# Attention and MoE on one core: the clip of the weight words on one engine, a second product buffer, and a new written-out order

## The chip, the cores and the metric

One core of one Trainium2 chip runs the whole program in one launch. The metric is device time in microseconds of one execution; the kernel before has a median of 686.51 us over 3 runs (685.51 to 687.27).

## The reference, cut to what matters

Rotary attention on 4 batches x 8 heads x 576 tokens x 64 dimensions, and then a two-layer MoE-like block on all 2304 tokens, with a sigmoid gate:

```python
q_rot, k_rot = rotate(q), rotate(k)                     # halves rotated by cos/sin of position
scores = scale * q_rot @ k_rot^T                        # (4, 8, 576, 576)
attn = exp(scores - max); attn /= sum + 1e-9
x = (attn @ v).transpose(0, 2, 1, 3).reshape(2304, 512)
h = x @ w_in                                            # (2304, 2048)
g = h / (1 + exp(-1.702 * h))
out = g @ w_out                                         # (2304, 512)
```

w_in and w_out are float64 in DRAM. The kernel reads them as pairs of 32-bit words and builds float32 values from them on the chip.

## The kernel before, in words

**Work.** The 32 heads are taken as 16 pairs (two heads of 64 dimensions fill the 128 partitions). For each pair, `scores` (L650) makes five steps of score products on TensorE (PE); `softened` takes each 128x576 row block through a scaling with row minimum on VectorE (L681, engine DVE), an exp on ScalarE (L684, ACT) and, from pair 4 on, a transpose on DVE (L689); `weighted` (L756) multiplies with v in two parts of 144 small matmuls each. Pairs 0 to 3 use other forms (`weighted_whole`: transposes L795 on PE, products L820 to L833). Results go to DRAM (`x_dram`), split into a high and a low float32r part.

**Weights.** `weight` (from L864) runs 32 times, 16 column blocks of w_in and 16 row blocks of w_out. Each run is a chain on one [128, 2, 512] buffer CW: L894 and L896 on ACT (low word to integer, absolute value of the high word), the clip L898 (a `tensor_scalar` with max and min), L900 and L903 on DVE (shift, sign), L906 on GpSimd (engine POOL; adds the low bits), then a rounding copy (L908) and a subtraction (L909).

**MoE.** Tokens go in 9 chunks of 256. For chunks 0 to 4 `moe` does, for each of 16 column blocks f: 12 matmuls "M" (L939) into one PSUM buffer h of the pool PT, tanh on ACT (L945), (t+1)h on DVE (L947), the high part g on ACT or POOL (L949), the low part on DVE or POOL (L951), and 2 x 3 matmuls "O" (L956) with w_out that accumulate in SPS buffer 2. Chunks 5 to 8 go in two calls of `two_chunks` (L1087, L1128), which shares products between two chunks. In the kernel before h always takes PT buffer 1 of two, and t and g have one buffer each (T=1, G=1 in SLOTS).

**Order.** Every step is an `Op` of a `Plan` of 3050 steps. Nothing is scheduled at run time: `PLACES` gives each step's place in one stream, `ENGINES` the engine of each step that may run on more than one (A, V, G for ACT, DVE, POOL), and `Plan.order` sorts by place and hands out buffers in that order. Each engine runs its part of the stream strictly in order, and SyncE (SP) issues nearly all DMAs in order too. `COST` holds prices in ns that went into such an order and do nothing at run time: a POOL step with one 128x512 source stands there at 121 + 0.97 x 512 = 618. One more wait is added by hand at the end of the loop: each POOL step that uses the port shared with DVE waits for the DVE step with the port mark that precedes it in the stream (`holder`).

Of the kernel before, what the change touches and what calls it, by code (L numbers as in the profile page):

```python
# [38 lines left out]
PLACES = [18, 0, 55, 26, 17, 23, 22, 12, 34, 1, 14, 52, 37, 28, 36, 35, 13, 24, 25, 30, 9, 6, 44, 10, 11, 45, 27, 57,  # L39
# [287 lines left out]
def attention_moe(ctx: ExitStack, tc: tile.TileContext, q, k, v, w_in, w_out, cos_sin, out):  # L327
# [589 lines left out]
    def moe(c, fs, t0, step):  # L917
# [9 lines left out]
        last = [None, None]  # L927
        for f_i in fs:
            pr = t0 + (f_i - fs[0]) * step
            h, t, g = plan.buf("PT", (1,)), buf("T"), buf("G")  # L930
            terms = [[(kk, 0, 0) for kk in range(KD)], [(kk, 1, 0) for kk in range(KD)],
                     [(kk, 0, 1) for kk in range(KD)]]
            if f_i == fs[-1]:
# [315 lines left out]
```

## Time and profile before

| what | us |
|---|---|
| median of 3 runs | 686.51 |
| the profiled execution, its own time | 684.21 |
| its span from the first to the last instruction | 682.5 |
| PE busy | 642.7 (94%) |
| DVE busy | 501.2 (73%) |
| ACT busy | 344.6 (50%) |
| POOL busy | 306.2 (45%) |

The stretches of the span are: warm-up matmuls (0 to 12), pairs 0 to 4 without MoE work (12 to 118), pairs 4 to 9 beside the MoE products of the first chunks and the last weights (118 to 300), pairs 9 to 15 beside the rest of chunks 2 to 4 (300 to 507), and the two shared calls (507 to the end). Busy time of PE is time in which some matmul was in flight, so a PE that is busy all the time may still run below its rate; the number of matmuls in a stretch tells how much work was in it. A wait is listed as "who <- for whom".

### The profile page before, as it was taken

What the parts mean: (1) busy time and instruction counts of PE and PEld (TensorE: products, weight loads), DVE (VectorE), ACT (ScalarE), POOL (GpSimd) and SP (SyncE); (2) the same over time, 40 slices, a digit from 0 to 9 for tenths busy, and PEclk for the clock granted to TensorE, in tenths of its full rate; (3) what the DMA queues carried; (4) which work ended last, traced back from release to release, by engine and by line L of the source; (5) the groups of instructions that cost most, each with busy time, mean ns of one, the idle gap of its engine ahead of it and who ended that gap; (6) DMA issues with size and microseconds to landing.
All of it is one profiled execution on the core that took longest, in us unless ns stands there. A gap on an engine that the chain in (4) does not pass through costs nothing.

```text
span 682.5 us, 18292 instructions
## 1 busy us (share of the span) xinstructions
PE 642.7 (94%) x7258; PEld 529.5 (78%) x7258; DVE 501.2 (73%) x1104; ACT 344.6 (50%) x839; POOL 306.2 (45%) x329
## 2 busy tenths in 40 slices
PE   8999887889889899989999999999999999999997
PEld 7655555767667687778878888888799899889886
DVE  4998779778799998877878988688375466544442
ACT  3987678265767655534354546446234323332232
POOL 3454547263566648654555557443012243133242
PEclk9999769889999999999999999999999999999999
DMA  7638464775688857666556747555446442343301
GB/s 194 151 81 202 122 189 142 207 143 182 170 225 230 225 136 218 194 181 168 175 147 178 192 138 214 137 137 153 139 163 202 148 149 89 124 130 118 124 0 63
DMA packets 82994, 107.16 MB, mean 157 GB/s; under 512 B 41254, under 2 KB 60892, under 8 KB 79708
## 3 DMA queue, kind: packets, MB, share of 16 engines
q1 hardware_dynamic: 81852, 105.73, 54.2%
q8 instruction: 57, 0.93, 0.6%
q10 hardware_dynamic: 1056, 0.26, 0.2%
q14 instruction: 29, 0.24, 0.1%
HBM read 71.68 MB, written 23.91 MB: 140 GB/s over the span
## 4 chain that ended last, share of the span: by engine, by line
PE 63%; DVE 17%; ACT 6%; issue 5%; POOL 3%; DMA 3%; SPq 1%; DVEq 0%; POOLq 0%; ACTq 0%
PE SPS L1128 13%; PE PT L939 12%; PE SPS L956 11%; PE SPS L650 7%; PE PT L1087 6%; PE SPS L1087 6%; PE SPS L756 5%; DVE TP L681 3%; DVE TP L689 2%; ACT TP L684 2%; POOL CW L898 2%; DVE CW L903 1%; PE SPS L443 1%; PE PT L795 1%; DMA XS<-r_dram 1%
## 5 line engine op out<-in xcount | busy, mean ns | idle before, releaser
L939 PE MATMUL PT<-XC,win 128*128 128x256 f32 x960 | 137.0, 289 | 5.9 <-DVE T L947 4.9
L939 PEld LDWEIGHTS PT<-XC,win 128*128 128x128 f32 x960 | 123.9, 190 | 21.9 <-DVE T L947 11.7
L956 PE MATMUL SPS<-wout,G 128*128 128x512 f32 x480 | 134.5, 407 | 4.0 <-DVE G L396 2.0
L684 ACT ACTIVATE TP<-TP,ST 128x576 f32<-128x576 f32 x144 | 111.0, 772 | 35.6 <-DVE TP L681 35.4
L681 DVE TENSOR_SCALAR_CACHE_REDUCE TP<-SPS 128x576 f32<-128x576 f32 x144 | 103.6, 747 | 19.5 <-PE SPS L650 19.0
L956 PEld LDWEIGHTS SPS<-wout,G 128*128 128x128 f32 x480 | 83.1, 190 | 26.1 <-DVE G L396 4.9
L1128 PE MATMUL SPS<-wout,G 128*128 128x512 f32 x384 | 97.0, 394 | 0.0
L689 DVE STREAM_TRANSPOSE TP<-TP 128x576 f32<-128x576 f32 x108 | 79.5, 760 | 2.2 <-ACT TP L684 2.1
L387 POOL TENSOR_SCALAR G<-T 128x256 fp32r<-128x256 f32 x64 | 28.5, 446 | 116.1 <-PE SPS L956 40.4
L1128 PEld LDWEIGHTS SPS<-wout,G 128*128 128x128 f32 x384 | 69.0, 188 | 13.0 <-ACT O L391 0.4
L396 POOL TENSOR_TENSOR G<-T,G 128x256 fp32r<-128x256 f32 x75 | 56.2, 753 | 50.2 <-DVE T L1119 13.8
L756 PE MATMUL SPS<-TP,VR 32*64 32x144 f32 x3456 | 62.9, 290 | 7.8 <-issue 6.4
L945 ACT ACTIVATE T<-PT 128x256 f32<-128x256 f32 x80 | 30.5, 381 | 78.6 <-PE PT L939 54.6
L906 POOL TENSOR_TENSOR CW<-CW 128x512 int32<-128x512 int32 x32 | 41.1, 1285 | 61.9 <-DVE CW L903 22.4
L756 PEld LDWEIGHTS SPS<-TP,VR 32*64 32x64 f32 x3456 | 55.9, 133 | 15.0 <-issue 9.2
L384 ACT CAST G<-T 128x256 fp32r<-128x256 f32 x80 | 32.2, 405 | 42.5 <-DVE T L947 14.0
L650 PE MATMUL SPS<-KH 64*128 64x288 f32 (+1 forms) x216 | 47.2, 345 | 5.4 <-DVE TP L681 5.0
L947 DVE SCALAR_TENSOR_TENSOR T<-T,PT 128x256 f32<-128x256 f32 x80 | 32.6, 407 | 22.9 <-ACT T L945 22.8
L1119 DVE SCALAR_TENSOR_TENSOR T<-T,U 128x256 f32<-128x256 f32 x64 | 28.3, 452 | 28.3 <-ACT T L1117 27.9
L650 PEld LDWEIGHTS SPS<-KH 64*128 64x128 f32 (+1 forms) x216 | 27.3, 189 | 20.5 <-DVE TP L681 10.1
L1117 ACT ACTIVATE T<-U 128x256 f32<-128x256 f32 x64 | 25.8, 417 | 34.2 <-DVE U L396 17.5
L898 POOL TENSOR_SCALAR CW<-CW 128x512 f32<-128x512 f32 x17 | 32.6, 1917 | 19.8 <-DVE RQ L396 4.6
(132 smaller groups left out, 1153.9 us busy)
## 6 DMA issues: line engine op xcount, KB each, us to landing
TR<-t_dram SPq DMA_DIRECT2D x16, 1024.0 KB
VR<-VR SPq DMA_DIRECT2D x36, 288.0 KB
x_dram<-XS SPq DMA_DIRECT2D x16, 576.0 KB
XC<-x_dram SPq DMA_DIRECT2D x18, 512.0 KB
OW<-in_moe_w_in_dram SPq DMA_DIRECT2D x16, 512.0 KB
OW<-in_moe_w_out_dram SPq DMA_DIRECT2D x16, 512.0 KB
RQ<-in_k_dram SPq DMA_DIRECT2D x40, 142.0 KB
RQ<-in_q_dram SPq DMA_DIRECT2D x40, 142.0 KB
```

The lines of the kernel that those rows point to most:

```text
L396: return engine[e].tensor_tensor(to, a, b, op=how)
L650: nc.tensor.matmul(ss[h].t[:, c, 0:HALF], of[x][rows, S + t * 128:S + t * 128 + 128], of[y][rows, c * HALF:c * HALF + HALF], start=(m == 0 ...
L681: o = vec("DVE", "psum", S, lambda e: nc.vector.tensor_scalar(tile_to(), src(), by, LARGEST, op0=ALU.mult, op1=ALU.min, accum_out=st.t[:, ...
L684: o = vec("ACT", "sbuf", S, lambda e: nc.scalar.activation(to(), to(), AF.Exp, bias=st.t[:, 0, t:t + 1], scale=-1.0, accum_out=st.t[:, 1, ...
L689: return o, vec("DVE", "psum", S, lambda e: nc.vector.transpose(to(), to()), o, bufs=[tp], prio=prio + at["exp"] + at["across"])
L756: nc.tensor.matmul(bank[64 * h:64 * h + 64, 0:144], vr.t[rows, h, a], of()[rows, a, 144 * h:144 * h + 144], start=(a == 0), stop=(a == n_k ...
L898: o = vec("DVE POOL", "sbuf", DM, lambda e, a=a: engine[e].tensor_scalar(a(), a(), clip[0], clip[1], op0=ALU.max, op1=ALU.min), o, bufs=[c ...
L906: o = vec("POOL", "two", DM, lambda e, a=a, r=r: nc.gpsimd.tensor_tensor(a().bitcast(I32), a().bitcast(I32), r(), op=ALU.add), o, low, buf ...
L939: nc.tensor.matmul(h.t[:, 0:CT], win[f_i // KH][:, wl, kk, f_i % KH * 128:(f_i % KH + 1) * 128], xc[xl].t[:, kk, :], start=(i == m == 0), ...
L956: nc.tensor.matmul(acc.t[:, m, :], g.t[:, a, m * 128:(m + 1) * 128], wout[f_i // KH][:, b, f_i % KH, :], start=(f_i == fs[0] and i == 0), ...
L1087: nc.tensor.matmul(h(to), w(a)[:, k], x(b)[:, k], start=(begin and n == 0), stop=(n == 5), skip_group_check=True)
L1128: nc.tensor.matmul(acc[j].t[:, m, :], g.t[:, x, m * 128:(m + 1) * 128], wout[f_i // KH][:, y, f_i % KH, :], start=(begin and n == 0), stop ...
```

## The change

Four edits. The clip L898 is issued on DVE in all 32 runs of `weight` (17 of them were on POOL). The MoE product h may take either of the two PT buffers instead of buffer 1 alone. The pool T gets two buffers instead of one. PLACES and ENGINES are replaced as a whole. No step is added or removed, and the line numbers stay.

```diff
-PLACES = [18, 0, 55, 26, 17, 23, 22, 12, 34, 1, 14, 52, 37, 28, 36, 35, 13, 24, 25, 30, 9, 6, 44, 10, 11, 45, 27, 57,
...
+PLACES = [10, 0, 38, 8, 4, 17, 7, 52, 20, 28, 55, 1, 41, 36, 29, 22, 15, 16, 14, 6, 23, 30, 9, 18, 5, 19, 43, 37, 44,
...
-SLOTS = dict(SPS=3, PT=2, RAW=2, RAW1=1, BT=1, KP=0, KH=1, KL=1, ST=2, CS=1, XS=1, XC=4, T=1, G=1, O=2, OW=2, CW=2, TP=1, VR=1)
+SLOTS = dict(SPS=3, PT=2, RAW=2, RAW1=1, BT=1, KP=0, KH=1, KL=1, ST=2, CS=1, XS=1, XC=4, T=2, G=1, O=2, OW=2, CW=2, TP=1, VR=1)
...
-        o = vec("DVE POOL", "sbuf", DM, lambda e, a=a: engine[e].tensor_scalar(
+        o = vec("DVE", "sbuf", DM, lambda e, a=a: nc.vector.tensor_scalar(
             a(), a(), clip[0], clip[1], op0=ALU.max, op1=ALU.min), o, bufs=[cv], prio=prio)
...
-            h, t, g = plan.buf("PT", (1,)), buf("T"), buf("G")
+            h, t, g = plan.buf("PT"), buf("T"), buf("G")
```

What the two pairs of lists say, counted step by step (sorting the steps by PLACES gives each engine's order, the letters of ENGINES its steps):

| steps | before | after |
|---|---|---|
| clip L898 on DVE / POOL | 15 / 17 | 32 / 0 |
| wide rope multiplication L516 on DVE / POOL | 14 / 2 | 9 / 7 |
| flat rope, L570 to L574, on DVE / POOL | 38 / 22 | 32 / 28 |
| high part of g, L949, on ACT / POOL | 48 / 32 | 56 / 24 |
| low part of g, L951, on DVE / POOL | 36 / 44 | 45 / 35 |
| weight differences L991 on DVE / POOL | 19 / 13 | 12 / 20 |
| copies out of PSUM in `two_chunks` L1095 on ACT / DVE | 46 / 18 | 33 / 31 |
| products M that follow the product before them with no other PE step between (of 79) | 0 | 37 |
| pairs O that start with three products M issued ahead of them (of 80; otherwise one or two) | 0 | 26 |
| PE steps between the two parts of `weighted` for pair 8 | M1.12, a transpose, half an O | half an O |

A stretch of PE's order around pair 8 (S: score step, M f.a to c: thirds of a product, O f.x and y: halves, V: a part of `weighted`, I: the transpose of the sums):

```
before: S8.4 M1.10c O1.9y O1.9x M1.11a M1.11b M1.11c O1.10x O1.10y V8.0 M1.12a M1.12b M1.12c I8 O1.11y V8.1 O1.11x S9.0
after:  S8.4 O1.9x M1.11c M1.12a M1.12b M1.12c O1.10x O1.10y V8.0 O1.11y V8.1 I8 O1.11x S9.0
```

Of the DVE steps that stand ahead of S9.0 in the stream, the after list has 17 more at L898 and 5 fewer at L516, and at the other lines between 2 fewer and 2 more each.

## Rows read from the trace of the kernel before

**Rows 1.** The page: busy shares, then PE's granted clock in 40 slices.

```profile
PE 642.7 (94%) x7258; PEld 529.5 (78%) x7258; DVE 501.2 (73%) x1104; ACT 344.6 (50%) x839; POOL 306.2 (45%) x329
...
PEclk9999769889999999999999999999999999999999
```

**Rows 2.** Windows: length, busy PE, PEld, DVE, ACT, POOL (instructions), clock, DMA.

```profile
12.00:118.00 106.00, 93.35 (x631) 58.88 (x629) 91.01 (x213) 85.97 (x202) 57.34 (x45) 0.92 0.56 149
118.00:300.00 182.00, 163.78 (x2448) 132.93 (x2449) 160.76 (x334) 105.10 (x247) 104.20 (x87) 0.97 0.72 197
300.00:507.00 207.00, 203.34 (x3051) 173.85 (x3051) 155.56 (x344) 93.35 (x235) 91.69 (x106) 1.00 0.58 163
...
160.00:200.00 40.00, 34.65 (x384) 27.25 (x387) 33.81 (x72) 26.08 (x61) 24.43 (x17) 1.00 0.72 206
200.00:250.00 50.00, 45.46 (x782) 36.13 (x766) 47.79 (x94) 32.95 (x77) 25.87 (x19) 1.00 0.72 201
...
650.00:675.00 25.00, 25.00 (x138) 21.60 (x137) 10.50 (x26) 7.32 (x20) 11.19 (x19) 1.00 0.03 11
```

**Rows 3.** Weight loads in 160 to 200, by line: L939, L956, L650, L756.

```profile
160.00:200.00 40.00, 12.22 (x99) 1.00 0.72 206
...
160.00:200.00 40.00, 8.01 (x48) 1.00 0.72 206
...
160.00:200.00 40.00, 4.67 (x54) 1.00 0.72 206
...
160.00:200.00 40.00, 2.81 (x185) 1.00 0.72 206
```

**Rows 4.** Chain of waits where PE is dense: start, us, what.

```profile
305.67 2.44 PE SPS L756 x144
...
492.24 1.39 PE SPS L956 x6
493.62 1.43 PE PT L939 x12
```

**Rows 5.** DVE's waits, first from 118 to 300, then whole: us, times, longest.

```profile
DVE CW L900 <- POOL CW L898: 9.2, 8, 1.8
...
DVE CW L900 <- POOL CW L898: 12.8, 10, 2.1
```

**Rows 6.** Timeline of DVE, then POOL: start, us, engine, line [idle before <- releaser].

```profile
160.41 1.40 DVE L900 TENSOR_SCALAR CW<-CW 128x512 int32<-128x512 int32 x1
...
169.70 0.43 DVE L900 TENSOR_SCALAR CW<-CW 128x512 int32<-128x512 int32 x1 [1.78 <-POOL CW L898]
...
160.09 1.44 POOL L906 TENSOR_TENSOR CW<-CW 128x512 int32<-128x512 int32 x1 [3.86 <-DVE G L396]
...
167.74 1.92 POOL L898 TENSOR_SCALAR CW<-CW 128x512 f32<-128x512 f32 x1 [2.31 <-DVE win L396]
```

**Rows 7.** The clip and rope by line and form: count, ns min/median/max; then groups, mean.

```profile
L898 POOL TENSOR_SCALAR CW<-CW x17: 1915/1917/1924, 20.5 to 232.9; 128x512 f32<-128x512 f32 x17
L898 DVE TENSOR_SCALAR CW<-CW x15: 414/426/1233, 24.1 to 245.3; 128x512 f32<-128x512 f32 x15
...
L898 DVE TENSOR_SCALAR CW<-CW 128x512 f32<-128x512 f32 x15 | 8.9, 596 | 1.3 <-ACT CW L896 1.3
...
L396 DVE TENSOR_TENSOR BT<-RAW,CS 128x512 f32<-128x512 f32 (+1 forms) x16 | 8.5, 534 | 5.0 <-DMA CS<-in_cos_sin_dram 5.0
```

**Rows 8.** Waits of PE's weight loads, whole span.

```profile
PEld PT L939 <- DVE T L947: 11.7, 18, 1.9
```

**Rows 9.** Timeline of PE: `weighted` for pair 4; a score step and its follower.

```profile
118.68 6.30 PE L756 MATMUL SPS<-TP,VR 32*64 32x144 f32 x278 [0.35 <-DVE TP L689]
128.22 0.48 PE L756 MATMUL SPS<-TP,VR 32*64 32x144 f32 x10 [3.24 <-issue]
...
313.98 0.40 PE L650 MATMUL SPS<-KH 64*128 64x288 f32 x2
...
314.98 1.66 PE L956 MATMUL SPS<-wout,G 128*128 128x512 f32 x6
```

More of the change, by code (lines that the diff above doesn't have):

```diff
@@ L38 @@
 MORE_TIMES = ['T_AT']
-PLACES = [18, 0, 55, 26, 17, 23, 22, 12, 34, 1, 14, 52, 37, 28, 36, 35, 13, 24, 25, 30, 9, 6, 44, 10, 11, 45, 27, 57,
[160 rows of a table removed]
-ENGINES = (".......................................VVV.A.VVV.VVV.VVV.A.........................A.A.A.A.A.A.A.A.A"
-           ".AA.AA..AA..A..VAV..GGG.V.VVG.AAA.VVG.A.........................V.A.A.A.A.A.A.A.A.AA.AA..AA..A..VVG."
-           ".VGV.A.VVG.AVA.GVV.A.........................V.A.A.V.A.A.A.V.A.AV.AV..VA..A..GVG..VVG.A.VGV.VAV.VVV."
-           "V.........................A.A.A.A.A.V.A.A.A.AA.AA..AA..A..GAG..VVG.A..VGG.V.V.V..VVV.A.............."
-           ".......................VVAV..A..VAV..VGV.A..VVV.V.A.V..VVV.A.....................................AAA"
-           "V..V..GAG..VGV.VV.VVV.AVAVAV....................................AVAV..A..GAG..GGG.AV.VVV.AVAVAV....."
-           "...............................AAVA..V..GAG..GVV.AV.VVV.AVAGAV....................................AA"
-           "AA..A..GVG..VGG.AG.GVV.VVVVVG....................................AAAV..A..GAV..GGG.AV.VGV.VVAGAV...."
-           "................................AAAA..A..VAV..VVG.AG.VVV.AVVVVG....................................V"
-           "AAA..V..GAG..GGG.VV.VVV.AVAGAV....................................AVAA..A..GAG..GVV.AG.VVV.VVVGVV..."
-           ".................................AAAA..V..GAG..GVG.AV.VVV.AVVVAV...................................."
-           "AAAA..V..GAG..VGG.AG.VGV.VVVVVV....................................AVVV..A..VAV....V...AV...V...AV.."
-           ".V...AG...V...AG...G...VG...G...AV...V...AV...V...AV...G...AV...V...VV...G...VV...G...AG...V...AG..."
-           "V...AG...G...AV...G...VV...V...AV...G...AV...G...AV...G...AG...V...AV...G...AV...G...AV...G...AV...V"
-           "...AV...G...AV...V...AV...G...AV...G...AG...G...AG...V...AV...V...AV.......GG.......GG.......AG....."
-           "..GG.......AG.......AV.......AV.......AV.............AV.......AV.......AV.......AV.......AG.......AV"
-           ".......AV.......AV.............AG.......AG.......AG.......AV.......AV.......AV.......AV.......AV...."
-           "...........AG.......GG.......GG.......AV.......AG.......AG.......AG.......AG...............AG......."
-           "GG.......GV.......AG.......GG.......AV.......GG.......GG.......GG.......GV.......AV.......AG.......A"
-           "G.......GV.......GG.......AG.............AG.......AV.......AV.......GG.......GG.......GG.......AG..."
-           "....GV.......GG.......AG.......GG.......GG.......GV.......AG.......GG.......GG.............GG......."
-           "GG.......AV.......GG.......AV.......GG.......GG.......AV.......AV.......AV.......GV.......GV.......G"
-           "V.......AV.......AV.......AV......GVVVGGAG.AV.VGGGGGAG.AV.GGVVVVVG.AG.GVVVVVVG.AG.GGGVVVAV.AV.VGVGVG"
-           "AG.AG.GGGGGGAV.AG.VVVVVVAG.AG.......VVVAVVVVAGVVAVVVVV..A.A.A..V..V......GV....AG....GV....GG....A.A"
-           ".A..G..A......AV....AV....GV....AG....A.A.A..V..A......GV....GG....AV....AV....V.A.A..G..A......AG.."
-           "..AG....AV....AG....V.V.A..G..V......AV....GV....GV....AG....A.A.A..V..A......GV....AG....GV....GV.."
-           "..V.A.A..G..A......AV....AV....GG....AV....A.A.A..G..V......GV....AG....AV....AV..A.A.V.V.......GVGV"
-           "VVVVAVGVAVGVAV..A.V.A..G..A......GV....GG....AV....AG....V.A.A..V..A......GG....GG....AG....GG....A."
-           "A.A..G..V......GV....GG....GV....AG....V.A.A..G..A......GV....AG....GG....GV....A.V.V..G..V......AG."
-           "...AV....GV....AV....V.A.A..V..V......AG....AV....GG....GG....V.A.A..G..A......AG....AG....GG....AG."
-           "...V.A.A..G..A......GV....GG....GV....GG..V.A.A.A.")
@@ L231 @@
-SLOTS = dict(SPS=3, PT=2, RAW=2, RAW1=1, BT=1, KP=0, KH=1, KL=1, ST=2, CS=1, XS=1, XC=4, T=1, G=1, O=2, OW=2, CW=2, TP=1, VR=1)
+PLACES = [10, 0, 38, 8, 4, 17, 7, 52, 20, 28, 55, 1, 41, 36, 29, 22, 15, 16, 14, 6, 23, 30, 9, 18, 5, 19, 43, 37, 44,
[160 rows of a table added]
+ENGINES = (".......................................VVV.A.VVV.VVV.VVV.A.........................A.V.A.A.A.A.A.A.V"
+           ".VA.AA..AA..V..VVV..VVG.A.VGG.AVA.VGG.V.........................A.V.A.A.A.A.A.A.A.AA.AA..AV..A..VAG."
+           ".GGV.A.GGG.VAV.GGV.A.........................A.A.A.V.A.V.A.A.A.VA.AV..AA..A..GAG..VVV.A.VVV.AAA.GVV."
+           "V.........................A.A.A.A.A.A.A.A.A.AA.AA..AA..A..GAG..GGG.A..VVV.V.V.V..VVV.A.............."
+           ".......................VVAA..V..VAV..GVV.V..VVG.A.V.V..GVV.V.....................................AVV"
+           "A..V..GAG..GGV.AV.VVV.AVVGAV....................................AAAV..V..GAG..GGG.AV.VVV.AVAVAG....."
+           "...............................AAAV..A..GAG..VGV.AV.VVV.AVVVAV....................................AV"
+           "AV..A..GAG..GGG.AV.VVV.AVAVAV....................................AAAV..V..GAG..GGG.AG.GVV.AVAVAV...."
+           "................................AAAA..A..GAV..VGG.AG.GGG.AVVVVV....................................A"
+           "AVA..A..GAG..VGG.AV.VVV.VVAGAV....................................AAVA..A..GVG..VVV.AG.VVV.AVVVAV..."
+           ".................................AVAA..V..GAG..GGG.AG.GVV.VGVVAG...................................."
+           "VVAV..A..GAG..VGG.AV.VGG.AGVGVG....................................VVAA..A..VVV........VG.......VV.."
+           ".....AV.......AG.......AG.......AV.......AV.......AV.......VV.......AV.......AV.......AV.......AV..."
+           "....AV.......AG.......VV.......AV.......AV.......AV.......AG.......AV.......AV.......AV.......AV...."
+           "...AV.......AV.......AG.......AV.......AG.......AG.......AV.......AV.......AG.......GV.......AG....."
+           "..GG.......AV.......AV.......AV.......AV.............AV.......GV.......AG.......AG.......AG.......AV"
+           ".......AV.......AV.............AG.......AG.......GG.......AV.......AV.......AV.......AV.......AV...."
+           "...........AG.......AG.......GG.......AV.......AG.......GV.......AV.......AG...............AV......."
+           "AV.......AG.......AV.......AV.......AG.......GG.......AG.......GV.......AV.......AV.......GG.......A"
+           "V.......AG.......AG.......GV.............GV.......AV.......AV.......AV.......AG.......GG.......AV..."
+           "....AG.......AG.......AG.......GG.......AV.......AV.......AG.......AV.......GG.............GG......."
+           "GG.......GV.......GG.......AG.......GG.......GV.......AV.......AG.......GV.......GV.......GV.......G"
+           "V.......AV.......AV.......AV......GGGGGGAG.AV.GGGGGGVG.AG.VGGVGVAV.VV.GVVVVGVV.AG.VGGGVVAV.AV.VGVVGG"
+           "AG.AG.GGGGGVAV.AV.VVGVVGAG.VV.......VVVAVVVVVVVVAVVVAV..A.A.A..G..A......AV....AV....GV....AG....A.V"
+           ".A..V..A......GV....AV....AG....GG....V.V.A..V..A......GG....GV....GG....GG....V.A.A..G..V......AG.."
+           "..AG....AG....GV....A.V.V..G..V......GG....GV....AV....AV....A.V.A..V..A......AV....AG....GV....AV.."
+           "..V.V.A..G..A......AV....AG....AV....GV....A.V.A..V..A......AG....GV....AV....GG..V.V.A.A.......GGVV"
+           "GGGVAVVVAGVGAV..V.V.V..V..A......AV....GG....AG....AV....V.V.V..V..V......GG....AG....AG....AV....V."
+           "V.A..V..A......GG....AG....GV....AG....A.V.V..V..V......GG....AG....GG....GV....A.A.A..V..A......GV."
+           "...GG....GV....GG....V.A.V..G..A......GV....AG....AV....AG....A.V.A..V..V......AG....GG....AV....AV."
+           "...V.V.A..V..V......GG....GV....GG....GV..V.A.A.A.")
```

320 rows, old and new, of the table PLACES are left out of this document.

## The prediction, on record before the changed kernel ran

> **What bounds the kernel now.** I read the page's busy shares first [rows 1]: PE is busy 94% of a span of 682.5 us, and the clock line shows nine full slices in ten; of the five slices from 68 to 154 us four are below 9 tenths. A busy PE need not be at its rate, so the windows come next, stretch by stretch [rows 2], and then the work in a stretch against its length. From 650 to 675 PE is busy 25.00 of 25 us, and in the dense middle a product M of 12 matmuls takes 1.43 us, an O-half pair of 6 takes 1.39, 144 small ones of `weighted` 2.44 [rows 4], and 12 score matmuls stand from 313.98 to 314.98, 1.0 us [rows 9]. With these prices the counts of 160 to 200 [rows 3] are 99 x 0.119 + 48 x 0.232 + 54 x 0.083 + 185 x 0.0169 = 11.8 + 11.1 + 4.5 + 3.1 = 30.5 us of work in 40 us. So there PE loses 9.5 us, though its busy row says only 5.35 is idle. In 118 to 300 DVE is busy 160.8 of 182 us (88.3%), in 200 to 250 47.8 of 50 (95.6%); PE is idle 18.2 us there, but 3.7 from 300 to 507, where DVE is at 75% [rows 2]. I conclude: before 300 us the in-order DVE sets the pace and PE waits for what it makes; after 300 PE itself is the bound.
>
> The waits of DVE say what keeps it from being full. In 118 to 300 it stands idle 21.2 us (182 - 160.8), and 9.2 of them, 8 times, are one wait: the shift L900 for the clip L898 on POOL; 12.8 over the whole span [rows 5]. The timeline shows how one comes about [rows 6]: POOL begins a clip at 167.74, after having idled 2.31 us for a DVE step, takes 1.92, and DVE stands 1.78 before L900 at 169.70.
>
> **The change, part by part.**
>
> Clip on DVE. Seventeen clips of 1917 ns leave POOL (32.6 us of POOL time) and cost DVE 426 ns each, 7.2 us in all [rows 7]. What is late next behind a clip is DVE itself, with no hand-over: L900 follows in its own queue. So the wait for POOL goes: 9.2 us in the stretch that DVE bounds. A clip on DVE can now wait for ACT's absolute value (L896), with everything behind it in DVE's queue; the trace has 1.3 us of that for 15 clips [rows 7], so 1.3 x 17 / 15 = 1.5 for all; it stays inside the bounds below.
>
> Port. The mean of DVE's clips is 596 ns against a median of 426, with one of 1233 [rows 7]; L900 once took 1.40 us, beside a POOL step that ran from 160.09 for 1.44 [rows 6], against 0.43 elsewhere. By the mean the 17 clips cost 10.1 us instead of 7.2. The other bound: POOL loses 17 of its longest steps, and whatever DVE time they stretched comes back; a like 2.9 us. I take zero between them.
> The Trainium skill, "SBUF — State Buffer", section "SBUF: two separate sides", says that VectorE and GpSimd share one pair of ports as an exclusive lock: the one that starts first keeps it for its whole instruction, and a VectorE instruction in a two-port mode or with two SBUF inputs is then fully blocked. The stretched L900 agrees. The rule speaks against the clip on DVE, since it makes 17 more instructions that can be blocked, and by it alone the dearer 10.1 us would stand.
>
> Other engine letters. Ahead of S9.0, the first score step of pair 9, DVE gets 17 clips more (7.2), 5 rope multiplications L516 fewer (5 x 0.534 = 2.7, [rows 7]), and the rest of the lines nearly cancel; I put them at +0.8, with two either way. DVE's work there is 5.3 us more. The later letters (L951 on DVE 9 times more, L991 7 times fewer, L1095 13 more) fall in stretches in which DVE has 25% and more to spare [rows 2]: nothing, unless PE's density breaks there.
>
> Second product buffer and T=2. With one buffer each, M(f+1) waits until L947 has read h of f. That is 11.7 us in 18 waits of PE's weight loads [rows 8]. In the new order 37 of 79 products follow the one before directly, and 26 times three are issued ahead. With g still in one buffer, an O pair can't come sooner; the freedom is that PE has a product to do while DVE is late. It can't make a DVE-bound stretch shorter than DVE's work, so I don't add it to the sum; it is why I trust PE to follow DVE's gain. Bounds: 0 and -11.7.
>
> Order. SP's queue and the early stretch are newly ordered. In 12 to 118 DVE is busy 91.0 and ACT 86.0 of 106 us, and PE at a mean clock of 0.92 [rows 2]. Clip waits of 12.8 - 9.2 = 3.6 us lie outside 118 to 300 [rows 5], and half of the new DVE clips would be 3.6 us of work: no change, bounds -4 and +4. After 300: bounds -3.7 (all idle gone) and +3.5 (a stall more like the 3.24 us of rows 9). The last 176 us: no change.
>
> Sum. If DVE runs 118 to 300 at the share that 200 to 250 shows, its 160.8 + 5.3 us take 166.1 / 0.956 = 173.7 us, 8.3 less than 182. The bounds are work against waits alone, 5.3 - 9.2 = -3.9, and, with half of PE's 11.7 on top of the 8.3, -14. I take -8.3, since the 95.6% row still has POOL clips in it [rows 7]. 684.21 - 8.3 = 675.9 for an execution like the profiled one (span 674.2). That one lies 2.3 us under the median of the runs, so 678.2 in the median.
>
> **The rivals.**
>
> *More comes along.* The new lists also win in the stretches that I hold still: 4 us before 118, 3.7 after 300: 8.3 + 7.7 = 16, or 670.5. For it: PE has 12.7 us idle in 12 to 118 besides its low clock. Against: DVE and ACT are both above 80% there, and their work is the same.
>
> *Code stalls eat it.* In pair 4, where both parts of `weighted` stand back to back, PE stood 3.24 us at "issue" after 278 of 288 matmuls [rows 9], waiting for nothing that the profile shows. The new order leaves only half an O between the parts of pair 8. Two such stalls at 3.24 are 6.5; the gain falls to 1.8 us, 684.7: the same. Against: pair 4 stands nearly so in both lists, and other parts are spaced. The Trainium skill, "Runtime: NRT & Kernel Launch", section "Instruction fetch mechanics", has the sequencer refill its code block by block in the background, mostly hidden; by that this rival has no price, but the 3.24 us are there.
>
> *DVE inherits the wait (slower).* Its queue is in order, so with 17 clips more it may only stand elsewhere: before L896, before the stretched POOL additions L906, before exps. Its share then stays at 88.3%, and 166.1 us of work take 188.1: 6.1 longer than now, 692.6. It decides where DVE's share of 118 to 300 stays below 166.1 / 182 = 91.3%. Against: in 200 to 250, where POOL still ran clips up to 232.9 us [rows 7], it reached 95.6%.
>
> *The clip was slack.* Transfers, not DVE, time the stretch to 300, and the gain turns into another wait: 686.5. For it: DVE's share looks full only where several chains meet; against: 9.2 of 21.2 idle us have one cause.
>
> **How the numbers follow.** The forecast 0.50 (its own range 674 to 683), more 0.18, code stalls 0.10, slack 0.08, DVE inherits 0.14. The range 668 to 690 takes in the first four and the milder half of the slower case; below it lies 0.08, above it 0.09. About 0.3%, 2.1 us, is what a measurement can tell: faster means under 684.4, same up to 688.6. Faster: 0.47 + 0.18 + 0.05 + 0.02 = 0.72. Slower: 0.11 + 0.03 = 0.14. Same: the rest, 0.14.
>
> **What would show it.** Right: no wait of L900 for L898; POOL busy near 280; DVE above 93% from the start of M0.0 to about S10; M's wait for L947 well below 11.7; the dense tail starts some 8 us before 507. Wrong: DVE's share unchanged with new waits before L898 or L906 (it inherits), more "issue" before L756 (code), or the same gap between the first M and the tail with DMA at its end (slack). If the gain lies before 118 us, the sum is right by luck.

## The result, and the profile after

The changed kernel takes 661.39 us in the median of 4 runs (658.38 to 663.25), against 686.01 (685.07 to 687.27) for the kernel before on the same chip: a ratio of 0.9636 [0.9596, 0.9676]. The forecast was 678.2 with a range from 668 to 690, so the sign was right and the time lies below the range. The profiled execution took 663.25 against 684.21 before, 21.0 us less.

The page of the changed kernel, first the busy shares, then the granted clock [rows 1]:

```profile
PE 628.3 (95%) x7258; PEld 523.9 (79%) x7258; DVE 501.8 (76%) x1133; ACT 341.5 (52%) x830; POOL 277.4 (42%) x309
...
PEclk9999998999999999999999999999999999999999
```

POOL is at 277.4, near the 280 forecast, and DVE at 501.8 does no more than the 501.2 of before, although it runs 17 clips more. Windows of the changed kernel, in the stretches and columns of [rows 2]:

```profile
12.00:118.00 106.00, 92.47 (x811) 59.77 (x811) 101.45 (x233) 87.61 (x203) 51.98 (x50) 0.97 0.60 165
118.00:300.00 182.00, 169.40 (x2533) 143.30 (x2514) 160.09 (x352) 108.37 (x256) 84.09 (x78) 0.99 0.76 204
300.00:507.00 207.00, 206.06 (x2953) 177.61 (x2952) 157.76 (x351) 97.57 (x250) 93.01 (x103) 1.00 0.56 160
160.00:200.00 40.00, 38.02 (x515) 31.07 (x513) 39.21 (x88) 28.35 (x68) 21.46 (x20) 1.00 0.80 211
200.00:250.00 50.00, 47.13 (x575) 39.54 (x573) 47.65 (x104) 34.79 (x81) 29.22 (x28) 1.00 0.79 208
```

In 160 to 200 DVE went from 33.81 to 39.21 of 40 us. In 12 to 118, held still in the forecast, it went from 91.01 to 101.45 of 106.

These windows lie at fixed times, while the work moves to earlier ones. So I also take the time at which PE begins the same product in each trace (matmuls counted along PE's written order) and cut the span there: the first MoE product M0.0, the first score step of pair 9 (S9.0), and the first product of the shared calls (the tail).

| us, in the profiled execution | M0.0 starts | S9.0 starts | tail starts | span |
|---|---|---|---|---|
| before | 129.0 | 278.5 | 507.6 | 682.5 |
| after | 121.2 | 259.0 | 486.7 | 661.5 |
| after, second chip (changed_again) | 121.4 | 258.1 | 483.8 | 658.6 |

By stretch, from before to after: start -7.8, M0.0 to S9.0 -11.7, S9.0 to the tail -1.4, tail -0.1; on the second chip -7.6, -12.8, -3.4 and -0.1. The forecast had 0, -8.3, 0 and 0. Windows cut at these marks, before:

```profile
0.00:129.00 129.00, 111.27 (x987) 75.83 (x988) 106.15 (x238) 91.03 (x210) 64.08 (x62) 0.92 0.58 156
129.00:278.50 149.50, 136.45 (x1892) 109.72 (x1890) 132.08 (x277) 90.17 (x211) 82.52 (x68) 0.98 0.73 196
278.50:507.60 229.10, 223.86 (x3320) 190.78 (x3321) 174.93 (x385) 106.26 (x267) 109.08 (x121) 1.00 0.59 166
```

And after:

```profile
0.00:121.20 121.20, 104.33 (x988) 70.62 (x988) 108.08 (x245) 90.86 (x207) 54.48 (x58) 0.97 0.61 166
121.20:259.00 137.80, 129.44 (x1898) 108.39 (x1891) 129.68 (x284) 89.84 (x210) 63.98 (x60) 1.00 0.81 212
259.00:486.70 227.70, 223.49 (x3319) 191.79 (x3320) 173.78 (x386) 106.33 (x272) 109.41 (x115) 0.99 0.59 168
```

Up to S9.0 DVE is busy 106.15 + 132.08 = 238.2 us before and 108.08 + 129.68 = 237.8 after. It is idle for 40.3 us before (278.5 - 238.2) and 21.2 after. So nearly all of the 19.5 us gained by then is idle time of DVE that is gone (19.1). Its waits from 118 to 300 in the changed kernel, the answer to [rows 5]:

```profile
DVE TP L681 <- PE SPS L650: 7.8, 7, 4.8
DVE CW L898 <- ACT CW L896: 2.9, 3, 1.7
DVE win L396 <- ACT win L384: 1.8, 1, 1.8
```

The wait of L900 for the clip is no longer there. What is late next, ACT's absolute value, costs 2.9 us. Two lines of DVE's timeline show a clip with its follower (start, us):

```profile
166.57 0.42 DVE L898 TENSOR_SCALAR CW<-CW 128x512 f32<-128x512 f32 x1
167.03 0.43 DVE L900 TENSOR_SCALAR CW<-CW 128x512 int32<-128x512 int32 x1
```

And PE's weight loads, over the whole span [rows 8]:

```profile
PEld PT L939 <- issue: 9.6, 39, 3.2
...
PEld PT L939 <- DVE T L947: 0.3, 1, 0.3
```

The products' wait for L947 fell from 11.7 us to 0.3, and "issue" is now what M's loads wait for most.

### The profile page after: what moved, and what is told of

It reads as the page before. It is cut to its first block, busy times and chain, and to the rows that moved or that the text cites. A ratio compares the mean times of both kernels' runs of the same rounds, so it can differ in the third digit from the quotient of the medians.

```text
span 661.5 us, 18243 instructions
## 1 busy us (share of the span) xinstructions
PE 628.3 (95%) x7258; PEld 523.9 (79%) x7258; DVE 501.8 (76%) x1133; ACT 341.5 (52%) x830; POOL 277.4 (42%) x309
## 4 chain that ended last, share of the span: by engine, by line
PE 70%; DVE 13%; ACT 6%; POOL 4%; issue 3%; DMA 3%; SPq 0%; DVEq 0%; POOLq 0%; ACTq 0%
PE SPS L1128 13%; PE PT L939 13%; PE SPS L956 12%; PE SPS L650 8%; PE SPS L756 8%; PE SPS L1087 6%; PE PT L1087 6%; DVE TP L681 3%; DVE TP L689 2%; PE SPS L820 2%; DVE CW L903 1%; ACT TP L684 1%; DMA OW<-in_moe_w_out_dram 1%; PE PT L795 1%; ACT TP L384 1%
## 5 line engine op out<-in xcount | busy, mean ns | idle before, releaser
L939 PE MATMUL PT<-XC,win 128*128 128x256 f32 x960 | 135.7, 288 | 3.4 <-issue 3.3
L939 PEld LDWEIGHTS PT<-XC,win 128*128 128x128 f32 x960 | 124.9, 190 | 15.0 <-issue 9.6
L956 PE MATMUL SPS<-wout,G 128*128 128x512 f32 x480 | 130.8, 401 | 1.8 <-issue 0.6
L956 PEld LDWEIGHTS SPS<-wout,G 128*128 128x128 f32 x480 | 83.2, 188 | 20.9 <-issue 3.4
L1128 PE MATMUL SPS<-wout,G 128*128 128x512 f32 x384 | 96.3, 394 | 0.0
L396 POOL TENSOR_TENSOR G<-T,G 128x256 fp32r<-128x256 f32 x68 | 50.0, 739 | 81.4 <-ACT G L384 37.9
L756 PE MATMUL SPS<-TP,VR 32*64 32x144 f32 x3456 | 63.3, 292 | 7.3 <-DVE TP L689 3.9
L756 PEld LDWEIGHTS SPS<-TP,VR 32*64 32x64 f32 x3456 | 56.0, 134 | 15.0 <-issue 6.5
L384 ACT CAST G<-T 128x256 fp32r<-128x256 f32 x89 | 35.9, 404 | 58.4 <-PE SPS L956 23.7
L387 POOL TENSOR_SCALAR G<-T 128x256 fp32r<-128x256 f32 x55 | 22.4, 410 | 99.2 <-DVE T L1119 27.4
L1117 ACT ACTIVATE T<-U 128x256 f32<-128x256 f32 x64 | 25.5, 416 | 46.7 <-DVE U L396 37.8
L650 PE MATMUL SPS<-KH 64*128 64x288 f32 (+1 forms) x216 | 45.0, 342 | 3.9 <-DVE TP L681 2.6
L396 DVE TENSOR_TENSOR G<-T,G 128x256 fp32r<-128x256 f32 x76 | 33.8, 449 | 17.1 <-POOL G L387 10.9
L650 PEld LDWEIGHTS SPS<-KH 64*128 64x128 f32 (+1 forms) x216 | 25.5, 186 | 17.8 <-DVE TP L681 7.4
L396 POOL TENSOR_TENSOR XS<-XS 128x576 fp32r<-128x576 f32 (+1 forms) x24 | 34.2, 1429 | 11.9 <-ACT XS L384 4.6
L650 PE MATMUL SPS<-KH,KL 64*128 64x288 f32 (+1 forms) x216 | 38.8, 300 | 0.0
```

The source lines that it names most:

```text
L384: return nc.scalar.copy(to, src)
L396: return engine[e].tensor_tensor(to, a, b, op=how)
L650: nc.tensor.matmul(ss[h].t[:, c, 0:HALF], of[x][rows, S + t * 128:S + t * 128 + 128], of[y][rows, c * HALF:c * HALF + HALF], start=(m == 0 ...
L756: nc.tensor.matmul(bank[64 * h:64 * h + 64, 0:144], vr.t[rows, h, a], of()[rows, a, 144 * h:144 * h + 144], start=(a == 0), stop=(a == n_k ...
L939: nc.tensor.matmul(h.t[:, 0:CT], win[f_i // KH][:, wl, kk, f_i % KH * 128:(f_i % KH + 1) * 128], xc[xl].t[:, kk, :], start=(i == m == 0), ...
L956: nc.tensor.matmul(acc.t[:, m, :], g.t[:, a, m * 128:(m + 1) * 128], wout[f_i // KH][:, b, f_i % KH, :], start=(f_i == fs[0] and i == 0), ...
```

## The experiments

Three theories were to be told apart for the 21 us: the clip on POOL (and if so, its hand-over to another engine or its length), the second buffers, and the new written order. In the kernels with only one part of the change the lists of before are adapted as far as the part needs it. In the rows of clip_only, edits_old_order and new_order_clip_back the lines of `weight` stand 7 further down: L905 is the clip, L907 the shift L900.

### clip_only: the kernel before, all 32 clips on DVE

```diff
-        o = vec("DVE POOL", "sbuf", DM, lambda e, a=a: engine[e].tensor_scalar(
+        o = vec("DVE", "sbuf", DM, lambda e, a=a: nc.vector.tensor_scalar(
```

> The kernel before with all 32 clips on DVE; its places, its other engine letters and its buffers stay. Theory H, the hand-over: the clip's trip to POOL and back held DVE in order (12.8 us of waits of L900 for L898), and most of the 21 us are this. Then the run takes 670 to 676 us, 10 us or more under the kernel before; the first MoE product starts several us before 129, the waits of L900 for L898 are gone and the granted clock of 65 to 118 us rises from 0.84. Theory O, the order: the old order was laid out around clips on POOL, and only a new order can use the freed time; then the run takes 681 to 687 us, DVE waits elsewhere by as much, and the first MoE product starts within 3 us of 129. Theory F, freedom: the second buffers carry the gain; then the same, 683 to 688.

Measured 673.69 us (670.32 to 676.07), ratio 0.9847 [0.9799, 0.9894]: the clip alone is worth some 11 us in the old order. Windows at its marks:

```profile
0.00:124.80 124.80, 105.91 (x987) 72.48 (x988) 106.54 (x245) 91.28 (x210) 50.57 (x55) 0.96 0.60 163
124.80:267.20 142.40, 133.98 (x1892) 109.46 (x1890) 134.75 (x287) 89.70 (x211) 62.53 (x58) 0.98 0.77 204
```

In the profiled executions the first product comes 4.2 us sooner. DVE's busy time up to S9.0 is 241.3 us, 3.1 more than before, and not 7.2 more.

### buffers_only and edits_old_order: the buffers alone, and the three edits, with the old order

```diff
-SLOTS = dict(SPS=3, PT=2, ..., T=1, G=1, ...
+SLOTS = dict(SPS=3, PT=2, ..., T=2, G=1, ...
...
-            h, t, g = plan.buf("PT", (1,)), buf("T"), buf("G")
+            h, t, g = plan.buf("PT", (1,) if (c, f_i) in [(1, 7), (2, 3)] else None), buf("T"), buf("G")
```

(The old stream has room for the other buffer in all products but these two.)

> The kernel before with T=2 and with the MoE product free to take either PT buffer, except for two of the 80 products whose place in the old order leaves them only buffer 1. Order, letters and clips stay. Theory F: the waits of PE's weight loads for L947 (11.7 us, 18 times) shrink to under 3 us and the run is 6 to 12 us faster, 674 to 680. Theories H and O: in the old order PE has no second product issued ahead, and where it waits it would wait for DVE's next step instead; the run is within 3 us of the kernel before, 683 to 688, although the waits for L947 shrink.

> The kernel before with the three small edits (clip on DVE, T=2, either PT buffer except for two products) and its own places and other letters. H: as the clip alone, 668 to 676. F: 672 to 678. O: 679 to 687; what is then missing to 661 is what the new lists are worth, 18 us or more.

Buffers alone: 686.04 us, ratio 1.0024 [1.0, 1.0049], no gain, although the waits of M's loads for L947 fall from 11.7 us to 3.2:

```profile
PEld PT L939 <- DVE T L947: 3.2, 4, 1.1
```

The three edits together: 675.07 us, ratio 0.9869 [0.9831, 0.9907], as clip_only. The 14 us from there to the changed kernel come with the new lists. (The kernel before was measured anew beside each group of runs, between 684.18 and 686.01 in the median, so a difference of medians of two groups can be off by 2 us. By the ratios, 0.9869 and 0.9636, the 14 us are 16.)

### new_order_clip_back: the changed kernel, the same 17 clips on POOL again

```diff
-        o = vec("DVE", "sbuf", DM, lambda e, a=a: nc.vector.tensor_scalar(
+        o = vec("DVE POOL", "sbuf", DM, lambda e, a=a: engine[e].tensor_scalar(
...
ENGINES at the 32 clip steps: the letters of before
```

> The changed kernel with the 17 clips that were on POOL put back there; the new places, the other new letters and both buffers stay. H: each clip takes 1.92 us on POOL instead of 0.42 on DVE and hands over twice, so nearly all is lost again: 676 to 685 us. O: the order does the work, the loss is what DVE's waits for L898 come to where they meet the bound, 663 to 670. F: as O.

Measured 681.92 us, ratio 0.9973 [0.9945, 1.0001]: without the clip on DVE the new order is worth nothing, and with it the clip on DVE is worth 20 us (681.92 - 661.39; 23 by the ratios). Its DVE waits for the clip, over the whole span:

```profile
DVE CW L907 <- POOL CW L905: 22.7, 12, 3.7
```

and the longest of them on the timeline of POOL, then of DVE:

```profile
167.99 3.94 POOL L905 TENSOR_SCALAR CW<-CW 128x512 f32<-128x512 f32 x2 [4.47 <-ACT G L391]
...
171.96 0.43 DVE L907 TENSOR_SCALAR CW<-CW 128x512 int32<-128x512 int32 x1 [3.69 <-POOL CW L905]
```

POOL waits 4.47 us for ACT and then has two clips in a row; DVE stands for nearly the whole of both.

### clip_back_short and old_order_short: the same hand-over, a shorter step

In each, the 17 steps on POOL stay where they are but multiply by 1.0 twice in place of max and min; the clip is left out there. The one is new_order_clip_back with this edit, the other the kernel before, its lists and buffers untouched.

```diff
-            a(), a(), clip[0], clip[1], op0=ALU.max, op1=ALU.min), o, bufs=[cv], prio=prio)
+            a(), a(), *((1.0, 1.0) if e == POOL else clip), op0=ALU.mult if e == POOL else ALU.max,
+            op1=ALU.mult if e == POOL else ALU.min), o, bufs=[cv], prio=prio)
```

> The changed kernel with the same 17 steps L898 on POOL as before, but there a multiplication by 1.0 twice instead of max and min (the clip is left out in these 17 of 32 runs; DVE clips as before in the others). Same hand-over, shorter step. The clip back on POOL took 681.9 us, the changed kernel 661.4. If the length of 1.92 us is what costs, a step of some 0.7 us gives back most: 663 to 670. If the hand-over from ACT to POOL to DVE costs (POOL must wait for DVE's last port step, DVE then for POOL), most of the loss stays: 673 to 682, and the waits of L900 for L898 stay above half of 22.7 us.

> The kernel before, its lists and buffers untouched; only the 17 clip steps on POOL become a multiplication by 1.0 twice (the clip itself is left out there). Theory LENGTH (in the old order too it is the 1917 ns of the POOL step that costs, not the hand-over to POOL and back): the step takes some 0.62 us as in clip_back_short, L900's waits for it fall from 9.2 to about 3 us in 118 to 300, and the time comes to what clip_only had, 672 to 677. HAND-OVER theory (in the old order L900 stands right behind the clip, so any POOL step there makes DVE wait, with no other step to fill the gap): at least half of the 12.8 us of waits stays and the time is 680 to 686.

In the new order: 662.61 us, ratio 0.969 [0.9657, 0.9723]; the step takes 623 ns in the median. On the same chip the changed kernel took 658.61 (changed_again below), so 4.0 us of the loss stay with a short step on POOL. In the old order: 669.3 us (665.93 to 673.23), ratio 0.9767 [0.9708, 0.9826], a little below what was expected. L898 in old_order_short by engine (count, ns min/median/max, first and last start), then its waits over the whole span:

```profile
L898 POOL TENSOR_SCALAR CW<-CW x17: 612/617/629, 20.5 to 217.5; 128x512 f32<-128x512 f32 x17
L898 DVE TENSOR_SCALAR CW<-CW x15: 414/420/1233, 24.2 to 228.5; 128x512 f32<-128x512 f32 x15
```

```profile
DVE CW L900 <- POOL CW L898: 1.9, 4, 0.8
```

So in both orders it is mostly the 1917 ns that cost, and not the hand-over: with the step still on POOL the waits fall from 12.8 us [rows 5] to 1.9. This kernel has DVE's instructions and order of before, so its windows show what else the length did (its profiled execution, at 666.31 us, is one of the two quicker of four):

```profile
0.00:121.60 121.60, 104.09 (x987) 71.16 (x988) 103.33 (x238) 90.96 (x210) 54.59 (x62) 0.99 0.62 166
121.60:261.00 139.40, 133.13 (x1892) 108.63 (x1890) 130.32 (x277) 89.51 (x211) 69.11 (x68) 0.99 0.79 210
261.00:489.60 228.60, 224.15 (x3319) 190.80 (x3320) 174.70 (x385) 106.06 (x267) 108.77 (x121) 1.00 0.59 167
```

The start shrinks by 7.4 us with no list touched, nearly as much as in the changed kernel. DVE's busy time up to S9.0 falls from 238.2 to 233.7 us, 4.6 less for the same instructions. Idle time falls from 40.3 to 27.3. Together these are the 17.5 us by which S9.0 comes sooner.

Where the 4.6 us come from can be read instruction by instruction, since DVE's list is the same in both. The lengths of single instructions (which overlap a little) add up to 3.9 us less. Only 0.3 of that is at instructions that ran beside a clip in the kernel before; 3.5 is at instructions that ran beside another POOL step. One of them, before and then in old_order_short, with the clip on POOL and the POOL step behind it (start, us):

```profile
51.13 1.92 POOL L898 TENSOR_SCALAR CW<-CW 128x512 f32<-128x512 f32 x1
...
53.02 1.45 POOL L396 TENSOR_TENSOR RAW<-RAW,BT 128x512 f32<-128x512 f32 x1
53.25 1.50 DVE L386 CAST wout<-CW 128x512 fp32r<-128x512 f32 x1
```

```profile
51.13 0.61 POOL L898 TENSOR_SCALAR CW<-CW 128x512 f32<-128x512 f32 x1
51.71 1.26 POOL L396 TENSOR_TENSOR RAW<-RAW,BT 128x512 f32<-128x512 f32 x1
...
53.19 0.41 DVE L386 CAST wout<-CW 128x512 fp32r<-128x512 f32 x1
```

After the long clip POOL's next step lies beside DVE's cast, which takes 1.50 us. After the short one that step is over before the cast begins, and the cast takes 0.41. So the clip itself stretches DVE little; here it delays the step behind it on POOL, and DVE is stretched beside that one.

### new_places_old_letters and old_places_new_letters: one list without the other

Clip on DVE and both buffers in each, and PLACES of after with ENGINES of before, or the reverse.

```diff
 PLACES = [10, 0, 38, ...        (after; before in the second kernel)
-ENGINES = (after)
+ENGINES = (before; after in the second kernel)
```

> The changed kernel with every engine letter as before, except the clips, which stay on DVE. Tells places from letters. If the places carry what the new lists are worth over the three edits (675 down to 661), 660 to 667 us; if the letters do (rope steps to POOL, low parts of g to DVE), 670 to 677; if only both together fit, over 675.

> The three edits with the old places (two of 80 products keep buffer 1) and all the new engine letters. Letters carry it: 661 to 668 us. Places carry it: 672 to 678. Only both fit together: over 678.

720.77 us, ratio 1.0527 [1.048, 1.0573], and 729.92 us (without its longest run, 739.15), ratio 1.0659 [1.0599, 1.0719]. The 14 us belong to neither list alone: these places and these letters gain only together.

### old_then_new: where the new lists gain

The steps up to the first MoE product in the order and with the letters of before, the rest as after; the clip on DVE.

```diff
-PLACES = [10, 0, 38, 8, ...
+PLACES = the order of before up to M0.0, then the remaining steps in the order of after
```

> The changed kernel, but with the old places and letters (clip on DVE) for all steps that the old list has ahead of the first MoE product; from there on the new lists. With the old order and the clips on DVE the first product starts at 125 us, in the changed kernel at 121. If the two parts add up, the first product starts near 125 and the run takes 4 us more than the changed kernel, 664 to 667. If the later part regains what the start lost (DVE is the bound there and has a store of work), 660 to 663. If the new start also leaves less work behind for DVE, over 668.

661.15 us, ratio 0.9655 [0.961, 0.97]. M0.0 starts at 124.0, 2.8 later than in the changed kernel, yet the whole is the same. So what the new lists win in the start can be had later too, and here their 14 us come from the steps behind it: M0.0 to S9.0 takes 138.2 us (143.3 in edits_old_order), S9.0 to the tail 224.0 (230.3).

### new_order_one_buffer and new_order_PT1: the new order without the second buffers

One buffer each for h and t, or only the second buffer for h taken away; the steps that this stops move to the next place that works (603 of 3050 in the second).

```diff
-            h, t, g = plan.buf("PT"), buf("T"), buf("G")
+            h, t, g = plan.buf("PT", (1,)), buf("T"), buf("G")
```

> The changed kernel with T=1 and the MoE product in buffer 1 alone, its places squeezed as little as that needs: a step that finds no free buffer waits in the list for the first place that has one, which leaves nearly the same order of PE. F, freedom to issue a product ahead: 668 to 676 us, with PE's waits for L947 back at 10 us. O, the order as such: 661 to 666, since DVE sets the pace before 300 us whether PE has a product ahead or not.

> The changed kernel with h of the products in PT buffer 1 alone, as before; T keeps its two buffers, and 603 of the 3050 steps move to the nearest places that this buffer allows. Theory PT (the new order's back-to-back products are carried by the second product buffer; T=2 only keeps tanh free): the next product's weight loads wait for L947 as in new_order_one_buffer (75 us in 52 waits there), 735 to 760. Theory T (it is the second tanh buffer that new_order_one_buffer lacked): at most 20 us of those waits, 661 to 680.

748.96 us, ratio 1.0921 [1.0863, 1.0979], and 725.25 us, ratio 1.0585 [1.0544, 1.0626]. The wait of M's loads for L947, in the first and then in the second:

```profile
PEld PT L939 <- DVE T L947: 75.1, 52, 3.6
```

```profile
PEld PT L939 <- DVE T L947: 57.0, 48, 3.6
```

The second PT buffer carries most of it: taking it away costs 64 us (725.25 - 661.39), the moves that this forces included. It came out a little below the 735 to 760 expected. T=1 by itself was not tried.

### spaced: more work between the two parts of `weighted` for pair 8

```diff
 order on PE around pair 8
-V8.0 O1.11y V8.1 I8 O1.11x S9.0
+V8.0 I8 O1.11y M1.13a M1.13b M1.13c V8.1 O1.11x S9.0
```

> The changed kernel with one product (M1.13) moved between the two parts of weighted for pair 8, and the transpose of pair 8's sums to right behind the first part. Every issue stall of PE in all traces so far begins at an instruction whose number on PE is 193 past a multiple of 256, and they come where two such blocks of 256 ran in under 6 us. Code theory: with 24 more instructions and 1.4 us between the two parts the stalls at 255.7 and 263.3 us (1.6 and 3.3 us) shrink to under 2 together, and the run is 2 to 4 us faster than the changed kernel, 657 to 660. If these stalls have another cause, or the next wait takes over, the same as the changed kernel within 1.5 us.

662.16 us, ratio 0.9687 [0.9657, 0.9718]: no gain, but some 3.5 us more than changed_again on the same chip (658.61). The first of the two stalls is gone. The second stands at the same instruction number as before, now ahead of S9.0, and takes 2.2 us; changed_again has 0.7 and 1.4 at the two places, so the sum is nearly the same.

### changed_again: the changed kernel once more

> The changed kernel unaltered, on the same chip as the one spaced out, for the comparison: 661 us, span 657 to 662, with issue stalls of 1.6 and 3.3 us near 255.7 and 263.3 us.

658.61 us (656.63 to 660.48), ratio 0.9635 [0.9608, 0.9661]: the result holds on a second chip. The two stalls expected at 1.6 and 3.3 us were 0.7 and 1.4 here. No kernel here beats it beyond its interval: with DVE relieved of the 17 clips (clip_back_short) nothing more comes.

## Why the prediction was right in sign and too small

DVE's time up to S9.0, from the windows at the marks (us; 40.3 = 278.5 - 238.2 and so on):

| kernel | S9.0 starts | DVE busy before it | idle before it |
|---|---|---|---|
| before | 278.5 | 238.2 | 40.3 |
| old_order_short | 261.0 | 233.7 | 27.3 |
| clip_only | 267.2 | 241.3 | 25.9 |
| edits_old_order | 268.6 | 241.5 | 27.1 |
| new_order_clip_back | 280.5 | 233.8 | 46.7 |
| clip_back_short | 260.3 | 232.8 | 27.5 |
| after | 259.0 | 237.8 | 21.2 |

**What bounds the kernel: right.** PE's instructions up to S9.0 are the same in before and old_order_short, and so are DVE's; only DVE's waits and durations shrank, and S9.0 came 17.5 us sooner. The tail kept its length (174.9 us before, 174.8 after).

**Clip: the right wait, the wrong cause.** The prediction named the wait of L900 and let it go; it went. It explained it by the hand-over to another engine's queue ("What is late next behind a clip is DVE itself, with no hand-over"). The short step keeps the hand-over and loses most of the wait (12.8 us to 1.9), so what was paid for is mainly the 1917 ns. What stays in the new order is the 4.0 us between clip_back_short and changed_again.

**Port: mis-sized, and the sign taken for zero.** The prediction bounded it at 2.9 us either way and took nothing. The clips themselves cost what it allowed: in the changed kernel the 32 on DVE take 17.4 us against 8.9 for 15, 8.5 more, between its 7.2 and 10.1. What it had too small is what comes back elsewhere: shortening the POOL step gave 4.6 us of DVE's busy time, more than its bound, and not where a clip lay beside DVE but where the POOL steps behind it did. So 17 clips more add 3.1 us of DVE's time in clip_only and not 7.2, and the "5.3 us more" ahead of S9.0 came out as 0.4 less. From M0.0 to S9.0 DVE's work fell by 2.4 us (132.08 to 129.68) at a share of 94.1%, a little under the 95.6% assumed; had the work risen as forecast, that share would not have given the stretch's 11.7 us. DVE's groups show it, in the changed kernel (busy us, mean ns):

```profile
L903 DVE SCALAR_TENSOR_TENSOR CW<-OW,CW 128x512 int32<-128x512 int32 x32 | 22.6, 711 | 0.3
L898 DVE TENSOR_SCALAR CW<-CW 128x512 f32<-128x512 f32 x32 | 17.4, 546 | 3.6 <-ACT CW L896 3.2
...
L900 DVE TENSOR_SCALAR CW<-CW 128x512 int32<-128x512 int32 x32 | 14.2, 449 | 0.5
```

against the kernel before:

```profile
L903 DVE SCALAR_TENSOR_TENSOR CW<-OW,CW 128x512 int32<-128x512 int32 x32 | 24.6, 769 | 0.3
L900 DVE TENSOR_SCALAR CW<-CW 128x512 int32<-128x512 int32 x32 | 16.2, 509 | 13.0 <-POOL CW L898 12.8
```

The clip's own mean on DVE is 546 ns, against 596 before [rows 7]. The longest clip on DVE still takes 1378 ns in the changed kernel, with a median of 422. The Trainium skill, "SBUF — State Buffer", section "SBUF: two separate sides", has VectorE and GpSimd hold a shared port pair one at a time, for a whole instruction. The runs agree with that in kind (a DVE cast of 0.41 us takes 1.50 beside a POOL step), but the prediction used the rule only against the change: a long step taken off GpSimd moves the steps behind it, and here gave VectorE back 4.6 us, about half of what the added clips cost.

**Start: the step that failed most.** "12 to 118: no change, bounds -4 and +4" came out as -7.8, outside its bounds, and is the largest part of the 12.7 us by which the sum fell short (21.0 - 8.3). It set 3.6 us of clip waits against 3.6 us of new clips, and took DVE's 86% and ACT's 81% for a limit. It was not one: old_order_short gives -7.4 there by the step's length alone: 2.8 us of DVE's busy time (106.15 to 103.33) and 4.6 us of its idle time. The stretch with the low clock is also in it. From 65 to 118, before, in old_order_short, and in new_order_clip_back:

```profile
65.00:118.00 53.00, 43.97 (x291) 28.33 (x290) 43.69 (x100) 39.35 (x90) 29.67 (x24) 0.84 0.54 150
```

```profile
65.00:118.00 53.00, 43.66 (x569) 30.04 (x568) 49.03 (x109) 40.13 (x92) 29.73 (x26) 0.97 0.61 180
```

```profile
65.00:118.00 53.00, 41.18 (x298) 25.57 (x296) 45.18 (x102) 41.13 (x92) 28.16 (x21) 0.96 0.54 153
```

PE's granted clock before is a mean of 0.84, so part of that time went by at the lower of its two levels (1.2 and 2.4 GHz); in old_order_short it is 0.97, and the same 53 us hold 569 matmuls instead of 291 (they reach further into the work). new_order_clip_back has 0.96 and yet starts its first product at 129.7, as late as before, with DVE busy for only 45.18 us: there a high clock alone gained nothing. How much of the 7.4 us the clock itself gave back, and how much DVE, these runs don't separate.

**Order and buffers: priced at nothing, worth 14 us together.** The prediction held the second buffers at 0 inside a stretch bound by DVE, which is right for the old order (ratio 1.0024). It said that they are "freedom", and left it there. But the new lists, which it counted only by their letters, gain some 14 us over the same edits in the old order. Between the profiled executions it is 12.4 us (673.9 and 661.5), of which 9.6 lie before S9.0 (DVE 3.7 us less busy and 5.9 less idle than in edits_old_order); in old_then_new half of it lies there (6.4 of 12.6). This order cannot be run without the second h buffer, whose loss costs 64 us with the moves that it forces.

**After 300 and the tail.** S9.0 to the tail gave 1.4 us (3.4 on the second chip), within the bounds of -3.7 and +3.5; the tail's zero was right.

**The rivals.** *DVE inherits the wait* fell: DVE's share from M0.0 to S9.0 is 129.68 / 137.8 = 94.1%, above its 91.3, and the new wait before L898 costs 2.9 us. *The clip was slack* fell with clip_only. *Code stalls* (their cause is not shown, see the last section) came at the place named, but not at its price: between the parts of `weighted` for pair 8 and behind S9.0 PE stands at "issue" for 1.58 and 3.27 us in the changed kernel,

```profile
255.73 1.03 PE L756 MATMUL SPS<-TP,VR 32*64 32x144 f32 x49 [1.58 <-issue]
...
263.30 2.33 PE L939 MATMUL PT<-XC,win 128*128 128x256 f32 x12 [3.27 <-issue]
```

and less than half of that in changed_again, whose profiled execution is 2.9 us shorter (660.35 and 663.25), about the difference of the stalls. *More comes along* had the signs right: both stretches held still gained, 7.8 and 1.4 us where it had 4 and 3.7. Its 670.5 was still 9 us too long, since the middle gained more too.

## What to carry to other kernels

A long instruction on a side engine is paid for in the wait of its reader, and again by what stands behind it in its own queue: those steps come later, and can then lie beside the neighbour's instructions and stretch them. The row of waits shows the first only (12.8 us here, where shortening the step gave 16.0). To learn which it is, keep the step where it is and make it short, before moving it. A buffer that is worth nothing in an order written for one may be what a better order stands on, so price order and buffers together, and engine letters together with places.

## What the runs showed of the hardware

**One operation, two lengths.** On POOL a `tensor_scalar` of 128x512 f32 takes 1917 ns with max and min [rows 7], and 617 ns with two multiplications, in the median. On DVE max and min take 422. Whether the max or the min makes it long on POOL was not tried.

**Stalls that begin at every 256th instruction, if at all.** In the traces before and after, PE's "issue" stalls above 0.5 us begin at an instruction whose number in PE's stream (matmuls, weight loads and the 70-odd semaphore instructions among them) is 193 plus a multiple of 256. The exceptions are stalls at instructions that wait for a semaphore whose releaser the profile does not name, the longest 2.44 us before L525 at 109.48 in the changed kernel. The stalls come only where the 256 instructions before took under 8 us, the stall counted, but in the changed kernel 21 of 26 such places have none. The expectation of spaced asked for two quick blocks in a row; the stall at 6337 before follows a block of 16.4 us. From the start of the instruction ahead to the start of this one:

```
before  1985: 3.5 us  6337: 2.5  7361: 0.9  7617: 1.2  12225: 0.5
after   1985: 1.3  4801: 1.1  5569: 1.9  5825: 3.3  8641: 1.0
```

The page has a queue that fits, in the changed kernel as before (packets, MB):

```profile
q8 instruction: 57, 0.93, 0.6%
```

57 x 256 = 14592, just above the 14589 instructions of PE's stream in the changed kernel (2 x 7258 of them matmuls and weight loads), and 0.93 MB / 57 is 16.3 KB, 64 bytes for each of 256. The Trainium skill, "Runtime: NRT & Kernel Launch", section "Instruction fetch mechanics", has the code come in blocks of this size; the runs agree. It calls the crossing mostly hidden; here single stalls cost up to 3.5 us, and spacing the work out only moved the stalls. That the stalls are code loading fits these numbers, but no run shows it.

**A gap can cost more than itself.** Behind the gap of 3.27 us in the changed kernel twelve matmuls of M took 2.33 us, against 1.43 in the dense middle [rows 4]. The granted clock is what changed. Ahead of the gap, and then behind it:

```profile
250.00:255.00 5.00, 4.08 (x179) 3.28 (x180) 4.86 (x11) 0.65 (x2) 0.00 (x0) 1.00 0.82 219
264.00:266.00 2.00, 2.00 (x12) 1.78 (x13) 0.00 (x0) 0.34 (x2) 0.15 (x1) 0.50 0.25 92
```

It is 1.00 and then 0.50, the lower of its two levels (1.2 and 2.4 GHz). In old_then_new, with a gap of 0.81 us ahead of the same product, the clock stayed at 1.00 and the twelve took 1.60.
